# Where two matrices' last columns are decoded: in the attention phase, or in the first steps of the token mix

## The chip, the cores and the metric

One core of a Trainium2 chip runs the kernel; the other cores take no part. The metric is the device time of one execution in microseconds. The kernel before has a median of 588.78 us over three runs (588.4 to 591.17). Names: TensorE is PE in the profile, VectorE is DVE, ScalarE is ACT, GpSimd is POOL, and SyncE, whose queue issues nearly all transfers, is SP.

## The reference

Two stages follow each other. The first is block-sparse attention over 4 batches of 8 heads, 768 positions of 64 elements: a query block of 32 positions sees its neighbours, the first and the last block and three drawn blocks, and the first and last query blocks see everything. The second takes the result as x (4 x 768 x 512):

```python
theta = x @ w_theta
zr, zi = x * np.cos(theta), x * np.sin(theta)
y = np.einsum('ts,bsd->btd', w_tok_r, zr) + np.einsum('ts,bsd->btd', w_tok_i, zi)
u = x + y
return u + np.maximum(u @ w_ch, 0.0)
```

The four weight matrices arrive as 64-bit floating-point numbers (float64 words), 128 partitions wide: w_theta and w_ch have 2048 columns per partition, w_tok_r and w_tok_i 4608 each (six row blocks j of 768). The kernel has to turn each into a pair of 32-bit matrices, a rounded high part and a remainder, and each product is three matmuls: high by high, high by low, low by high.

## The kernel before

**Decoding.** Class `Piece` (L49) turns a run of columns of one matrix into the pair. A piece is loaded as raw words (`raw`, SP, L62), and its work is cut into three phases. *bits* is three VectorE instructions (L71, L72, L73) behind a ScalarE one (L67); *rest* is two on VectorE (L79, L81); *low* is two on VectorE (L90, L91) behind a ScalarE copy that writes the high part (L87). `Decoder` (L94) walks through a list of pieces: `ahead(n)` issues ScalarE's part of the next n phases, `go(n)` VectorE's. Two raw buffers exist, so `go` issues the load of the piece after next behind a *low* (L122).

**Attention.** It works through 52 units: for each of two batch pairs, four wide ones (the first and last query blocks) and 22 regular ones. In a regular unit TensorE makes scores S (L308), VectorE their row minimum m (L310), ScalarE the exponentials P (L319), TensorE transposes them (L325), ScalarE copies the result to pT (L327), and TensorE multiplies with the values into X (L359). Every second unit VectorE normalises two blocks (L340 to L344). GpSimd gathers keys (L269) and values (L291). All of this stands in an order written out by hand, and the engines follow it. Here the first decoder runs: w_theta (4 pieces of 512 columns), then w_tok_r and w_tok_i (9 each). Its 66 phases are dealt out over the units in proportion to weights, by rounding (L493):

```python
phases = round(shares[n] / total * 3 * len(pieces)) - decoder.at
```

A regular unit gets one phase or two. The columns of the token matrices from 1536 on have no place of their own: they are written over buffers that hold keys and values until attention has no more use for them.

**Token mix.** `token_mix` (L585) runs 48 steps k: batch b, half h of the channels, row block j. What a step issues runs ahead of it: `theta(k + 2)` is the matmul with w_theta (L654 to L656), whose left side are the token rows, transposed (`turn`, L637) and cut into two parts (`split`, xTh and xTl, L645 and L646); `reduced`, `waves` and `turned` make the factors zh and zl (L664 to L690); `mix(k)` multiplies them with row block j of the token matrices (L706 to L708). At j = 5 the sum is finished (`add_x`, L713), and `out` (L724) multiplies with w_ch, eight tiles a batch; the tiles of batch 0 are issued in the steps from 13 on. The loads of the tokens, `xa` (L609, four transfers a step) and `xr` (L622), go through SP's queue, in order.

A second decoder takes w_ch in eight pieces of 256 columns. Its first two loads are issued near the end of attention. Steps 0 to 4 (`FIXED`) are part of the hand-written order and run 1, 1, 1, 3 and 3 phases; from step 5 on a scheduler sets the order by its own estimate of times, and three phases are issued in each step from 7 on until all are done.

Of the kernel before, what the change touches and what calls it, by code (L numbers as in the profile page):

```python
# [26 lines left out]
Q_BUFS = 3  # L27
XO_BUFS = 2
FIXED = 5
PHASES = (1, 1, 1, 3, 3)  # L30

# [551 lines left out]
def token_mix(tc, w, ch_pieces, xs, outT, bias, nb, fore):  # L585
# [7 lines left out]
    nc = tc.nc  # L593
    with ExitStack() as late, ExitStack() as ctx:
        half_pi, up_int, down_int, early = bias
# [3 lines left out]
        def at(k):  # L599
            return k // 12, (k // 6) % 2, k % 6  # L600
# [26 lines left out]
        def turn(k, tag="r"):  # L627
            b, h, j = at(k)
            if h:
                return  # L630
            if j % 3 == 0:
                tp = tps[min((2 * b + j // 3) % 3, 1)]
                xT[b, j // 3] = [tp.tile([P, 4, 384], F32R, tag=f"xT{x}", name=f"xT{x}{b}_{j}") for x in "hl"]
            raw = xr.pop((b, j))
            turning[k] = r = xp.tile([P, 4, 128], F32, tag=tag, name=f"r{k}", bufs=3 if tag == "xa" else 1)
            for c in range(4):
                nc.vector.transpose(r[:, c, :].rearrange("p (i t) -> p i t", t=32), raw[:, :, c])  # L637
# [10 lines left out]
        def theta(k):  # L648
            b, h, j = at(k)
            hi, lo = tok(b, j)  # L650
            wh, wl = [x[:, :, 256 * h : 256 * h + 256] for x in w["theta"]]
            angles[k] = ps = ps_h.tile([P, 512], F32, tag="h", name=f"h{k}")[:, 0:256]
            for c in range(4):
                nc.tensor.matmul(ps, hi[:, c, :], wh[:, c, :], start=c == 0, stop=False)  # L654
                nc.tensor.matmul(ps, hi[:, c, :], wl[:, c, :], start=False, stop=False)  # L655
                nc.tensor.matmul(ps, lo[:, c, :], wh[:, c, :], start=False, stop=c == 3)  # L656
# [11 lines left out]
        def waves(k):  # L668
            r = angles[k]
            cs = tz.tile([P, 256], F32, tag="cs", name=f"cs{k}")  # L670
            nc.scalar.activation(cs, r, AF.Abs)  # L671
            nc.scalar.activation(cs, cs, AF.Sin, bias=half_pi, scale=-1.0)
            nc.scalar.activation(r, r, AF.Sin)
            angles[k] = cs, r
# [17 lines left out]
        def turned(k):  # L692
            multiplied(k)
            highs(k)
            lows(k)
# [43 lines left out]
        place = vp.tile([P, 6, 260], F32, tag="vw", name="xr_first").rearrange("p c f -> p (c f)")  # L739
# [5 lines left out]
        decoder = Decoder(ch_pieces(), None, nc.sync, fore)  # L745
# [40 lines left out]
        for k in range(FIXED):  # L786
            theta(k + 2)
            waves(k + 1)
            turn(k + 3)
            turned(k + 1)  # L790
            split(k + 3)
            reduced(k + 2)
            load(k + 3)
            load_raw(k + 5)
            phases = PHASES[k] if k < len(PHASES) else 0
            decoder.ahead(phases)
            decoder.go(phases)
            mix(k)
# [4 lines left out]
        for k in range(FIXED, steps):  # L803
            b, h, j = at(k)
            if k + 4 < steps:
                load(k + 4)
            if k + 5 < steps:
                load_raw(k + 5)
            if k + 2 < steps:
                theta(k + 2)  # L810
                reduced(k + 2)
                waves(k + 2)
                turned(k + 2)
            if k + 3 < steps:
                turn(k + 3)
                split(k + 3)
            if k > 6 and decoder.left():
                decoder.ahead(3)
                decoder.go(3)
            mix(k)  # L820
            if h == 0 and b > 0 and 0 < j < 5:
                for _ in range(2):
                    out(*pending.pop(0), ps_o, "o")
            if h == 1 and j == 5:
                pending += [(b, th, e) for th in range(2) for e in range(4)]
# [4 lines left out]
def sparse_attention_then_token_mix(ctx, tc, qT, qE, kT, vr, sampled, w_theta, w_tok_r, w_tok_i, w_ch, outT):  # L830
    nc = tc.nc
    n_batch = outT.shape[0]
    const = ctx.enter_context(tc.tile_pool(name="const", bufs=1))
    ident = const.tile([P, P], F32, name="ident")
    make_identity(nc, ident)
    bias = []
    for name, value in (("half_pi", math.pi / 2), ("up_int", ROUND), ("down_int", -ROUND), ("early", 0.0)):
        bias.append(const.tile([P, 1], F32, name=name))
        nc.vector.memset(bias[-1], value)
    dram = ctx.enter_context(tc.tile_pool(name="dram", bufs=1, space=bass.MemoryType.DRAM))  # L840
    xs = [dram.tile([NB, 2, 32, 2, 2, P], F32, name=f"xs{bp}") for bp in range(NP)]

    w = {}
    w["theta"] = [const.tile([P, 4, 512], F32R, name=f"w_theta_{x}") for x in ("hi", "lo")]
    for name in ("tok_r", "tok_i"):
        w[name] = [const.tile([P, 2, 768], F32R, name=f"w_{name}_{x}") for x in ("hi", "lo")]

    def room(name, use, dtype=F32):
        return const.tile([P, 8, 768], dtype, tag=f"room_{name}", name=f"{use}_{name}")

    def settle(name):
        t = room(name, "w", F32R)
        w[name] = [x[:, j] for x in w[name] for j in range(2)]
        w[name] = [w[name][2 * x : 2 * x + 2] + [t[:, 4 * x + j] for j in range(4)] for x in range(2)]
        return [t[:, 4 * x : 4 * x + 4] for x in range(2)]

    words = {n: a.bitcast(I32) for n, a in dict(theta=w_theta, tok_r=w_tok_r, tok_i=w_tok_i, ch=w_ch).items()}

    def pieces(name, f, place, at=0, total=3072):
        if place:  # L860
            total = place[0].shape[1] * place[0].shape[2]
        made = []
        for f0 in range(0, total, f):
            made.append(Piece(nc, place, slice(f0, f0 + f), words[name][:, 2 * (at + f0) : 2 * (at + f0 + f)], f"{name}_{at + f0}"))
        return made


    fore = ctx.enter_context(tc.tile_pool(name="fore", bufs=2))
    follow = token_mix(tc, w, lambda: pieces("ch", 256, w["ch"], total=2048), xs, outT, bias, n_batch, fore)
    next(follow)  # L870
    early = pieces("theta", 512, w["theta"])
    early += [x for pair in zip(pieces("tok_r", 512, w["tok_r"]), pieces("tok_i", 512, w["tok_i"])) for x in pair]
    for name in ("tok_r", "tok_i"):
        place = []
        early += pieces(name, 512, place, 1536)
        early[-6].before = lambda name=name, place=place: place.extend(settle(name))
    attention(tc, qT, qE, kT, vr, sampled.bitcast(I32), xs, ident, early, room, follow)
    for _ in follow:
        pass
# [48 lines left out]
```

## Time and profile before

The profiled execution is one of its own: 592.62 us, with a span of 590.8 us from the first instruction to the last, at a mean TensorE clock of 0.991.

| | busy, us | share of the span |
|---|---|---|
| TensorE, matmuls | 538.4 | 91% |
| TensorE, weight loads (beside them) | 475.3 | 80% |
| VectorE | 442.8 | 75% |
| ScalarE | 342.7 | 58% |
| GpSimd | 148.6 | 25% |

Attention is the first 246 us or so; the first product of `mix(0)` starts at 252.9 us. GpSimd works in the first part alone. A busy share is a mean over both parts, so the table by itself says little: the prediction goes by stretches.

In the profile's rows `out<-in` are tile names without their numbers, `x9` is a count, and behind the bar stand the busy time in us, the mean of one instruction in ns, and the idle time of the engine before it with what ended it. A timeline row is start, duration, engine, line, operation. A row of waits is the total, the count and the longest.

### The profile page before, as it was taken

The page shows a single profiled execution, that of the slowest core. Times are in us where ns is not written, and L with a number is a line of the kernel's source. Part 1 is how long each engine was busy: PE and PEld are TensorE (multiplying, and loading weights), DVE is VectorE, ACT ScalarE, POOL GpSimd, SP SyncE. Part 2 cuts the span into 40 slices and gives each one's busy share as a digit, 9 for nine tenths or more (in the row PEclk, how much of TensorE's full clock was granted, in tenths as well). Part 3 has the DMA queues.
Part 4 walks back from the last instruction along what each step waited for, and adds up shares of the span by engine and source line. Part 5 has one row for each costly group of instructions (what it writes and reads, how often), then busy time and mean ns, then how long its engine had stood idle before and what let it go on. Part 6 is the DMA issues. An engine that isn't in the chain of part 4 may idle for free.

```text
span 590.8 us, 16785 instructions
## 1 busy us (share of the span) xinstructions
PE 538.4 (91%) x6636; PEld 475.3 (80%) x6636; DVE 442.8 (75%) x997; ACT 342.7 (58%) x730; POOL 148.6 (25%) x262
## 2 busy tenths in 40 slices
PE   4897878888977977999999999999999999999997
PEld 2564555656645645799999999999999999999996
DVE  3788788878897988888989976648857549547554
ACT  2677666868776876865657443456634547434510
POOL 1477758841775977000000000000000000000000
PEclk9999998999998989999999999999999999999999
DMA  8979999886698998644332341211432111212002
GB/s 293 340 223 344 308 332 348 287 267 223 185 299 257 304 307 225 193 121 131 108 85 76 96 130 59 72 45 54 130 92 70 50 53 42 80 56 75 2 1 107
DMA packets 63263, 95.60 MB, mean 162 GB/s; under 512 B 9168, under 2 KB 44624, under 8 KB 63184
## 3 DMA queue, kind: packets, MB, share of 16 engines
q1 hardware_dynamic: 56848, 71.09, 39.0%
q0 software_dynamic: 6336, 23.43, 12.2%
q8 instruction: 52, 0.85, 0.6%
q14 instruction: 27, 0.22, 0.1%
HBM read 81.90 MB, written 12.58 MB: 160 GB/s over the span
## 4 chain that ended last, share of the span: by engine, by line
PE 68%; DVE 15%; ACT 8%; issue 4%; DMA 4%; SPq 1%; ACTq 0%; DVEq 0%
PE y L706 11%; PE y L707 11%; PE y L708 11%; PE X L359 4%; PE o L730 4%; PE o L729 4%; PE o L731 4%; PE T L325 4%; DVE m L310 3%; PE h L655 3%; PE h L654 3%; PE h L656 3%; ACT P L319 3%; PE S L308 3%; PE SW L401 2%
## 5 line engine op out<-in xcount | busy, mean ns | idle before, releaser
L319 ACT ACTIVATE P<-S,m 128x256 f32<-128x256 f32 x176 | 69.5, 487 | 15.2 <-DVE m L310 15.2
L325 PE MATMUL T<-ident,P 128*128 128x128 f32 x352 | 50.9, 285 | 15.0 <-ACT pT L327 10.4
L310 DVE TENSOR_REDUCE m<-S 128x4 f32<-128x1024 f32 x44 | 53.6, 1217 | 12.3 <-PE S L308 12.3
L327 ACT COPY pT<-T 128x1024 f32<-128x1024 f32 x44 | 44.9, 1021 | 30.5 <-PE T L325 30.4
L325 PEld LDWEIGHTS T<-ident,P 128*128 128x128 f32 x352 | 38.8, 143 | 27.8 <-ACT pT L327 18.3
L291 POOL DMA_INDIRECT vb<-in_vr_dram,rows x44 | 46.3, 1052 | 48.8 <-PE X L359 43.3
L308 PE MATMUL S<-kg,q 64*32 64x256 f32 x1408 | 52.8, 394 | 5.9 <-issue 5.9
L661 ACT ACTIVATE t<-h,up_int 128x256 f32<-128x256 f32 x48 | 22.6, 474 | 59.7 <-PE h L656 56.0
L269 POOL COPY kg<-kb 128x256 f32 (+2 forms) x101 | 50.9, 544 | 15.8 <-PE S L308 15.8
L269 POOL COPY kg<-kb_tok_i 128x256 f32 (+2 forms) x101 | 49.4, 530 | 21.1 <-DMA kb_tok_i<-in_kT_dram 14.9
L654 PE MATMUL h<-w_theta_hi,xTh 128*128 128x256 f32 x192 | 54.1, 282 | 0.4 <-ACT xTh L645 0.4
L656 PE MATMUL h<-w_theta_hi,xTl 128*128 128x256 f32 x192 | 54.1, 282 | 0.2 <-DVE xTl L646 0.2
L655 PE MATMUL h<-w_theta_lo,xTh 128*128 128x256 f32 x192 | 53.9, 281 | 0.0
L706 PE MATMUL y<-w_tok_r,zh 128*128 128x384 f32 x128 | 43.1, 337 | 1.1 <-ACT zh L686 1.1
L706 PE MATMUL y<-w_tok_i,zh 128*128 128x384 f32 x128 | 43.1, 337 | 0.0
L707 PE MATMUL y<-w_tok_r,zh 128*128 128x384 f32 x128 | 43.1, 337 | 0.0
L707 PE MATMUL y<-w_tok_i,zh 128*128 128x384 f32 x128 | 43.1, 336 | 0.0
L708 PE MATMUL y<-w_tok_r,zl 128*128 128x384 f32 x128 | 43.0, 336 | 0.0
L730 PE MATMUL o<-ul,w_ch_hi 128*128 128x384 f32 x128 | 42.9, 335 | 0.0
L731 PE MATMUL o<-uh,w_ch_lo 128*128 128x384 f32 x128 | 42.9, 335 | 0.0
L729 PE MATMUL o<-uh,w_ch_hi 128*128 128x384 f32 x128 | 42.6, 336 | 0.1
L671 ACT ACTIVATE cs<-rr 128x256 f32<-128x256 f32 x48 | 19.7, 414 | 39.1 <-DVE rr L666 38.9
(155 smaller groups left out, 1427.4 us busy)
## 6 DMA issues: line engine op xcount, KB each, us to landing
xa<-xs SPq DMA_DIRECT2D x192, 64.0 KB
out_dram<-of SPq DMA_DIRECT2D x32, 192.0 KB
va<-in_vr_dram SPq DMA_DIRECT2D x22, 260.0 KB
q<-in_qT_dram SPq DMA_DIRECT2D x22, 256.0 KB
xs<-xo SPq DMA_DIRECT2D x88, 64.0 KB
xr<-xs SPq DMA_DIRECT2D x84, 64.0 KB
raw_tok_r<-in_w_tok_r_dram SPq DMA_DIRECT2D x9, 512.0 KB
raw_tok_i<-in_w_tok_i_dram SPq DMA_DIRECT2D x9, 512.0 KB
```

The lines of the kernel that those rows point to most:

```text
L269: nc.gpsimd.tensor_copy(dst, blocks.rearrange("r g s f -> r s g f"))
L308: nc.tensor.matmul(sc[32 * p : 32 * p + 32, e, b, :], q[rows, b, p, :], keys[rows, :, :, place(b, p), :], start=True, stop=True)
L310: nc.vector.tensor_reduce(m, sc, axis=AX.X, op=ALU.min)
L319: nc.scalar.activation(pt[:, e, b, :], sc[:, e, b, :], AF.Exp, bias=m[:, e, b : b + 1], scale=-1.0)
L325: nc.tensor.transpose(t[:, k, :], pt, ident)
L654: nc.tensor.matmul(ps, hi[:, c, :], wh[:, c, :], start=c == 0, stop=False)
L655: nc.tensor.matmul(ps, hi[:, c, :], wl[:, c, :], start=False, stop=False)
L656: nc.tensor.matmul(ps, lo[:, c, :], wh[:, c, :], start=False, stop=c == 3)
L706: nc.tensor.matmul(acc, zh[:, dd], wh[j][:, tt], start=j == 0 and m == 0, stop=False)
L707: nc.tensor.matmul(acc, zh[:, dd], wl[j][:, tt], start=False, stop=False)
L708: nc.tensor.matmul(acc, zl[:, dd], wh[j][:, tt], start=False, stop=j == 5 and m == 1)
L730: nc.tensor.matmul(ps, wh[:, c, :], ul, start=False, stop=False)
```

## The change

The last 512 columns of w_tok_r and of w_tok_i (columns 4096 to 4607, the greater part of row block 5) leave the first decoder. They become four pieces of 256 columns at the head of the second decoder's list, in front of the eight pieces of w_ch. The first decoder has 20 pieces and 60 phases instead of 22 and 66, dealt out over the same units; the second has 12 pieces and 36 phases. `PHASES` now names steps 0 to 12: the token columns take the first twelve phases, which end with step 3, and w_ch takes the rest, up to step 12. The two loads near the end of attention now fetch columns of w_tok_r. All lines from L30 on move down by one.

```diff
-PHASES = (1, 1, 1, 3, 3)
+PHASES = (2, 3, 3, 4, 4, 0, 4, 4, 4, 3, 3, 0, 2)
+LATER = 2560
...
-            phases = PHASES[k] if k < len(PHASES) else 0
+            phases = PHASES[k]
             decoder.ahead(phases)
             decoder.go(phases)
             mix(k)
...
-            if k > 6 and decoder.left():
-                decoder.ahead(3)
-                decoder.go(3)
+            if k < len(PHASES):
+                decoder.ahead(PHASES[k])
+                decoder.go(PHASES[k])
             mix(k)
...
-    follow = token_mix(tc, w, lambda: pieces("ch", 256, w["ch"], total=2048), xs, outT, bias, n_batch, fore)
+    rests = dict(tok_r=[], tok_i=[])
+
+    def mix_pieces():
+        made = [x for n, place in rests.items() for x in pieces(n, 256, place, 1536, (LATER, 3072))]
+        return made + pieces("ch", 256, w["ch"], span=(0, 2048))
+
+    follow = token_mix(tc, w, mix_pieces, xs, outT, bias, n_batch, fore)
...
-    for name in ("tok_r", "tok_i"):
-        place = []
-        early += pieces(name, 512, place, 1536)
-        early[-6].before = lambda name=name, place=place: place.extend(settle(name))
+    for name, place in rests.items():
+        made = pieces(name, 512, place, 1536, (0, LATER))
+        made[0].before = lambda name=name, place=place: place.extend(settle(name))
+        early += made
```

How the instructions move, first on VectorE in attention, late in the first batch pair: from the minimum of unit 20's scores to that of unit 22's. Before:

```order
L310 TENSOR_REDUCE m_20_2018<-S_20_2001 128x4
L71 TENSOR_SCALAR da_tok_i_1999<-da_tok_i_1999 128x512
L72 TENSOR_SCALAR da_tok_i_1999<-da_tok_i_1999 128x512
L73 SCALAR_TENSOR_TENSOR da_tok_i_1999<-raw_tok_i_1815,da_tok_i_1999 128x512
L340 TENSOR_SCALAR sm_17_2089<-X_17_2020 128x8
L341 RECIPROCAL sm_17_2089<-sm_17_2089 128x8
L344 TENSOR_TENSOR xo_17_2092<-X_17_2020,sm_17_2089 128x512
L310 TENSOR_REDUCE m_21_2122<-S_21_2105 128x4
L79 TENSOR_SCALAR ds_tok_i_2139<-da_tok_i_1999 128x512
L81 SCALAR_TENSOR_TENSOR raw_tok_i_1815<-raw_tok_i_1815,ds_tok_i_2139 128x512
L90 TENSOR_TENSOR da_tok_i_1999<-da_tok_i_1999,w_tok_i_hi 128x512
L91 TENSOR_TENSOR w_tok_i_lo<-da_tok_i_1999,raw_tok_i_1815 128x512
```

And of the change, from unit 18's minimum to behind that of unit 20:

```order
L311 TENSOR_REDUCE m_18_1840<-S_18_1823 128x4
L80 TENSOR_SCALAR ds_tok_i_1908<-da_tok_i_1770 128x512
L82 SCALAR_TENSOR_TENSOR raw_tok_i_1572<-raw_tok_i_1572,ds_tok_i_1908 128x512
L341 TENSOR_SCALAR sm_15_1911<-X_15_1842 128x8
L342 RECIPROCAL sm_15_1911<-sm_15_1911 128x8
L345 TENSOR_TENSOR xo_15_1914<-X_15_1842,sm_15_1911 128x512
L311 TENSOR_REDUCE m_19_1951<-S_19_1934 128x4
L91 TENSOR_TENSOR da_tok_i_1770<-da_tok_i_1770,w_tok_i_hi 128x512
L92 TENSOR_TENSOR w_tok_i_lo<-da_tok_i_1770,raw_tok_i_1572 128x512
L311 TENSOR_REDUCE m_20_2005<-S_20_1988 128x4
```

Where two units carried three phases (seven decode instructions), some pairs of units now carry two.

Second, VectorE in the mix, from `reduced(3)` in step 1 to the `split(5)` of step 2, which `theta(5)` on TensorE waits for. Before:

```order
L666 TENSOR_SCALAR rr_4742<-rr_4742 128x256
L79 TENSOR_SCALAR ds_ch_4751<-da_ch_4672 128x256
L81 SCALAR_TENSOR_TENSOR raw_ch_4261<-raw_ch_4261,ds_ch_4751 128x256
L637 STREAM_TRANSPOSE r_4795<-xr_5_4667 128x128 x4
L681 TENSOR_TENSOR cs_4791<-cs_4791,xa_4662 128x256
L681 TENSOR_TENSOR rr_4742<-rr_4742,xa_4662 128x256
L690 TENSOR_TENSOR zl_3_4803<-cs_4791,zh_3_4802 128x256
L690 TENSOR_TENSOR zl_3_4805<-rr_4742,zh_3_4804 128x256
L646 TENSOR_TENSOR xTl_3_4637<-r_4795,xTh_3_4636 128x4x128
```

Of the change:

```order
L667 TENSOR_SCALAR rr_4719<-rr_4719 128x256
L91 TENSOR_TENSOR da_tok_r_4646<-da_tok_r_4646,w_tok_r 128x256
L92 TENSOR_TENSOR w_tok_r<-da_tok_r_4646,raw_tok_r_4235 128x256
L72 TENSOR_SCALAR da_tok_r_4729<-da_tok_r_4729 128x256
L73 TENSOR_SCALAR da_tok_r_4729<-da_tok_r_4729 128x256
L74 SCALAR_TENSOR_TENSOR da_tok_r_4729<-raw_tok_r_4237,da_tok_r_4729 128x256
L80 TENSOR_SCALAR ds_tok_r_4738<-da_tok_r_4729 128x256
L82 SCALAR_TENSOR_TENSOR raw_tok_r_4237<-raw_tok_r_4237,ds_tok_r_4738 128x256
L638 STREAM_TRANSPOSE r_4782<-xr_5_4641 128x128 x4
L682 TENSOR_TENSOR cs_4778<-cs_4778,xa_4636 128x256
L682 TENSOR_TENSOR rr_4719<-rr_4719,xa_4636 128x256
```

Step 1 had one phase (two instructions) in front of the next step's work, and now has three (seven); the two rows on zl and the split follow as before.

More of the change, by code (lines that the diff above doesn't have):

```diff
@@ L857, in sparse_attention_then_token_mix, with pieces @@
     words = {n: a.bitcast(I32) for n, a in dict(theta=w_theta, tok_r=w_tok_r, tok_i=w_tok_i, ch=w_ch).items()}
-    def pieces(name, f, place, at=0, total=3072):
-        if place:
-            total = place[0].shape[1] * place[0].shape[2]
+    def pieces(name, f, place, at=0, span=None):
         made = []
-        for f0 in range(0, total, f):
-            made.append(Piece(nc, place, slice(f0, f0 + f), words[name][:, 2 * (at + f0) : 2 * (at + f0 + f)], f"{name}_{at + f0}"))
+        first, last = span or (0, place[0].shape[1] * place[0].shape[2])
+        for f0 in range(first, last, f):
+            f1 = min(f0 + f, last)
+            made.append(Piece(nc, place, slice(f0, f1), words[name][:, 2 * (at + f0) : 2 * (at + f1)], f"{name}_{at + f0}"))
         return made
     fore = ctx.enter_context(tc.tile_pool(name="fore", bufs=2))
-    follow = token_mix(tc, w, lambda: pieces("ch", 256, w["ch"], total=2048), xs, outT, bias, n_batch, fore)
+    rests = dict(tok_r=[], tok_i=[])
[3 more added lines that the diff above has]
+    follow = token_mix(tc, w, mix_pieces, xs, outT, bias, n_batch, fore)
     next(follow)
```

## The prediction

> **What bounds the kernel now.** I read the page's slices first, then busy time by stage, then what TensorE waits for, then the chain of waits.
>
> ```profile
> span 590.8 us, 16785 instructions
> PE   4897878888977977999999999999999999999997
> DVE  3788788878897988888989976648857549547554
> DMA  8979999886698998644332341211432111212002
> ...
> core 0: us, PE busy (x) PEld busy (x) DVE busy (x) ACT busy (x) POOL busy (x), PEclk, DMA share, GB/s
> 0.00:246.00 246.00, 199.97 (x4439) 138.67 (x4440) 197.75 (x336) 173.51 (x324) 148.57 (x262) 0.98 0.89 281
> 246.00:345.00 99.00, 96.75 (x701) 95.34 (x700) 88.08 (x263) 60.95 (x154) 0.00 (x0) 1.00 0.37 105
> 345.00:591.00 246.00, 241.64 (x1501) 241.32 (x1500) 156.97 (x400) 108.25 (x253) 0.00 (x0) 1.00 0.21 65
> ...
> PE y L706 <- ACT zh L686: 1.1, 1, 1.1
> ...
> 252.90 0.41 PE L706 MATMUL y<-w_tok_r_hi,zh 128*128 128x384 f32 x1 [0.34 <-DVE xo L344]
> ```
>
> There are two programs in one. Attention (to about 246 us) has no full engine: TensorE 200.0, VectorE 197.8, ScalarE 173.5 of 246, and the DMA engines at 0.89. The mix behind it, whose first product starts at 252.90, is TensorE's: the list of its waits from there on holds one of 1.1 us and that one of 0.3, so whatever is moved there is free only while VectorE and ScalarE stay ahead. Until 345 us they hardly are: VectorE is busy 88.08 of 99. After 345 it has 246 - 157 = 89 us to spare.
>
> In attention the chain of waits changes hands. Two stretches, and VectorE's busy time in those where it carries the chain:
>
> ```profile
> by line: DVE m L310 34.5%; DVE da_tok_i L73 11.1%; DVE da_tok_i L71 8.2%; DVE da_tok_i L90 7.6%; DVE w_tok_i L91 7.3%; DVE raw_tok_i L81 7.3%; DVE da_tok_i L72 7.3%; DVE xo L344 6.9%; DVE ds_tok_i L79 3.9%; issue 2.4%; ACT P L319 2.4%; DVE
> by line: PE X L359 21.1%; PE S L308 20.0%; PE T L325 19.1%; issue 13.3%; ACT pT L327 8.4%; ACT P L319 7.5%; DVE m L310 7.2%; PE X L366 3.5%; DVE da_tok_i L90 1.8%; DVE w_tok_i L91 0.8%; ACTq L327 0.1%
> ...
> 28.00:52.00 24.00, 21.78 (x36) 1.00 0.82 247
> 105.00:124.00 19.00, 17.39 (x28) 1.00 0.87 270
> 186.00:206.00 20.00, 19.41 (x30) 1.00 0.94 285
> ```
>
> The first row is the chain from 186 to 206 us: half of it (11.1 + 8.2 + 7.6 + 7.3 + 7.3 + 7.3 + 3.9 = 52.7%) is decoding of w_tok_i. There VectorE is busy 19.41 of 20 us, and a phase less is time less. The second row is 206 to 240 us: scores, transposes and values carry it, and decoding has 2.6%. So VectorE sets the pace in about 63 of the 210 us that decode.
>
> **The change, part 1: what leaves attention.** Two pieces of 512 columns, one of each token matrix, with their two loads of 512 KB. What one costs:
>
> ```profile
> L73 DVE SCALAR_TENSOR_TENSOR da_tok_i<-raw_tok_i,da_tok_i 128x512 int32<-128x512 int32 x9 | 6.6, 738 | 0.3
> L81 DVE SCALAR_TENSOR_TENSOR raw_tok_i<-raw_tok_i,ds_tok_i 128x512 f32<-128x512 uint32 x9 | 6.5, 726 | 0.3
> L91 DVE TENSOR_TENSOR w_tok_i<-da_tok_i,raw_tok_i 128x512 fp32r<-128x512 f32 x6 | 5.6, 940 | 0.3
> L71 DVE TENSOR_SCALAR da_tok_i<-da_tok_i 128x512 f32<-128x512 f32 x9 | 5.0, 551 | 2.4 <-ACT da_tok_i L67 2.4
> L90 DVE TENSOR_TENSOR da_tok_i<-da_tok_i,w_tok_i 128x512 f32<-128x512 f32 x6 | 4.6, 773 | 0.0
> L79 DVE TENSOR_SCALAR ds_tok_i<-da_tok_i 128x512 int32<-128x512 int32 x9 | 4.4, 487 | 0.1
> L72 DVE TENSOR_SCALAR da_tok_i<-da_tok_i 128x512 int32<-128x512 int32 x9 | 4.2, 468 | 0.3
> ...
> L310 DVE TENSOR_REDUCE m<-S 128x4 f32<-128x1024 f32 x44 | 53.6, 1217 | 12.3 <-PE S L308 12.3
> ```
>
> VectorE: 738 + 726 + 940 + 551 + 773 + 487 + 468 = 4.68 us a piece, 1.56 us a phase. So 9.4 us of VectorE go, and ScalarE's two instructions a piece. But 60 phases instead of 66 are dealt out over the same units, so it is not the last stretch that empties: by the rounding, 14 units lose a phase and 8 gain one, six fewer in all. One net phase falls into each of the three full stretches quoted: 3 x 1.56 = 4.7 us. The other three fall where TensorE, instruction issue or a transfer carries the chain; I give them 0.2 us each. Sum **-5.3 us**. Bounds: if only one full stretch pays, -1.5. At the other end, the 44 row minima (L310) mark the units' starts: of 19 pairs of regular units, the 15 with three phases took 9.2 us on the mean, the 4 with two 7.1. That is 2.1 us a phase, and six of them -12.5 us. I stay near the low end because the longer pairs also hold the waits for transfers, which no phase causes. The loads (2 x 512 KB at 281 GB/s, 3.7 us of a DMA queue that is 0.89 busy) pull the same way and are not counted again.
>
> **Part 2: what comes to the mix.** The same columns in four pieces of 256, before any of w_ch, so that steps 0 to 4 now run 16 phases instead of 9 and w_ch ends in step 12.
>
> ```profile
> L81 DVE SCALAR_TENSOR_TENSOR raw_ch<-raw_ch,ds_ch 128x256 f32<-128x256 uint32 x8 | 3.4, 422 | 0.1
> L73 DVE SCALAR_TENSOR_TENSOR da_ch<-raw_ch,da_ch 128x256 int32<-128x256 int32 x8 | 3.4, 420 | 0.1
> L90 DVE TENSOR_TENSOR da_ch<-da_ch,w_ch_hi 128x256 f32<-128x256 f32 x8 | 3.4, 420 | 0.2 <-ACT xTh L645 0.2
> L91 DVE TENSOR_TENSOR w_ch_lo<-da_ch,raw_ch 128x256 fp32r<-128x256 f32 x8 | 3.4, 419 | 0.0
> L71 DVE TENSOR_SCALAR da_ch<-da_ch 128x256 f32<-128x256 f32 x8 | 2.3, 291 | 2.1 <-ACT da_ch L67 2.1
> L79 DVE TENSOR_SCALAR ds_ch<-da_ch 128x256 int32<-128x256 int32 x8 | 2.3, 289 | 0.1
> L72 DVE TENSOR_SCALAR da_ch<-da_ch 128x256 int32<-128x256 int32 x8 | 2.2, 284 | 0.0
> ```
>
> A piece is 2.55 us by its durations. In the queue instructions overlap a little: in the timeline below, the six from L72 to the next stage's L681 take 280.33 - 278.12 = 2.21 us, with L71 about 2.4, or 0.8 a phase. Four pieces are 9.6 us (10.2 by durations) on an engine that was idle 99 - 88 = 11 us until 345. All of it fits by then; the question is what it delays on the way.
>
> ```profile
> 266.33 0.69 DVE L646 TENSOR_TENSOR xTl<-r,xTh 128x512 fp32r<-128x512 f32 x1
> 278.12 0.25 DVE L72 TENSOR_SCALAR da_ch<-da_ch 128x256 int32<-128x256 int32 x1
> 280.33 0.42 DVE L681 TENSOR_TENSOR cs<-cs,xa 128x256 f32<-128x256 f32 x1
> 290.41 0.42 DVE L690 TENSOR_TENSOR zl<-rr,zh 128x256 fp32r<-128x256 f32 x1
> ...
> 268.55 0.28 PE L656 MATMUL h<-w_theta_hi,xTl 128*128 128x256 f32 x1
> 291.65 0.51 PE L708 MATMUL y<-w_tok_i_hi,zl 128*128 128x384 f32 x2
> ...
> DVE r L637 <- DMA xr<-xs: 1.4, 2, 0.9
> ```
>
> First place: theta(5). Its token rows are ready at 266.33 + 0.69 = 267.02 and first used at 268.55, 1.5 us in hand. By the order VectorE now has five phases ahead of them instead of two, 3 x 0.8 = 2.4 us more, so TensorE stands 0.9. Second place: mix(6). Its last factor is ready at 290.41 + 0.42 = 290.83 and used at 291.65, 0.8 in hand. Ahead of it, counted from mix step 0, the order has 36 decode instructions where there were 23, seven to a piece: 13/7 x 2.4 = 4.5 us. The two waits for raw x rows (1.4) are swallowed, because VectorE comes later to them. That leaves 4.5 - 0.8 - 1.4 = 2.3 us, in which the 0.9 is contained. TensorE's 1.1 us stall of before comes behind this place and is partly covered by it, so I take **+2.0 us**. Behind the late instructions queue the next stage's multiplications and, in order, all of mix(7) to mix(12). Lower bound 0, if VectorE's other short waits go too; upper bound +7, all 9.6 us less the 0.8 in hand, the 1.4 and a part of the old stall.
>
> Two more things are late next.
>
> ```profile
> 317.22 0.42 DVE L91 TENSOR_TENSOR w_ch_lo<-da_ch,raw_ch 128x256 fp32r<-128x256 f32 x1
> ...
> 342.16 0.34 PE L729 MATMUL o<-uh,w_ch_hi 128*128 128x384 f32 x1
> ...
> 296.02 0.44 ACT L67 ACTIVATE da_ch<-raw_ch 128x256 f32<-128x256 f32 x1 [3.41 <-DMA raw_ch<-in_w_ch_dram]
> ```
>
> The last piece of w_ch was ready at 317.6, and the first output tile that needs it began at 342.16, 24 us in hand. Now it is due in step 12, and the order has it behind the factors of mix(14): a few microseconds stay, and I cost it at nothing. The four added loads go through SP's queue, each behind the VectorE instruction that frees its buffer, and the loads of xa and xr behind it wait too. The third row shows the worst that was: ScalarE stood 3.41 us for a raw piece. In the new order the third to sixth load are issued in steps 1 to 3, a step ahead of their use; I count 0 to 0.6 us, inside the +2.0.
>
> The Trainium skill's page "VectorE: DVE Perf Modes" (section "The TRN2 errata — SBUF-src ops pay a fixed extra latency per instruction") speaks against halving the pieces: every instruction pays a fixed cost, and it advises 512 elements or more. The trace agrees in the durations, 2 x 2.55 = 5.09 us for two halves against 4.68 for a whole. By the rule the exchange costs 2 x 0.4 = 0.8 us of VectorE time more, and the sum below would end at -2.5; I go by the 2.4 us that a piece holds the queue, where that cost is mostly overlapped.
>
> **Sum.** -5.3 + 2.0 = -3.3 us. Made against the profiled execution (592.6 us by its own time, span 590.8) this is 589.3. That execution lies 3.8 above the median of the runs, which I forecast as 588.8 - 3.3 = **585.5 us**.
>
> **Rivals.**
> A. VectorE paces all of attention: the 2.1 us a phase of the pairs is real everywhere. -10 to -12.5, +2.0: about 579.5. For it: decode is half of VectorE's work there. Against: the chain from 206 to 240 us.
> B. Attention does not follow VectorE: its end is set by TensorE's 200 us, by transfers (0.89 busy) and by issue, and the freed time reappears as waits for scores. -1.5 to -2 and +2: 588.8. For it: the second chain row. Against: 19.41 of 20.
> C. Slower: VectorE's queue from the end of step 1 to mix(6) becomes the bound. If its waits there are not swallowed, because they are ScalarE's latencies and late raw pieces, the whole upper bound of +7 falls on TensorE; with -4 from attention that gives +3, 592 us. It decides if theta(5) already comes over 2 us late, where I count 0.9. For it: 88 of 99 us busy. Against: before, steps 3 and 4 ran three phases each without a stall.
> D. The order doesn't do what the table says: after step 4 a scheduler places the phases, and if VectorE is 4 us later than I count, the last w_ch piece holds the output matmuls of step 13. Those 4 us on top: 589.5.
>
> **Chances.** Forecast 0.45 (its own range 582.8 to 587.8), A 0.13, B 0.27, C 0.13, D 0.02. What a measurement can tell here is about 0.5%, 2.9 us. Faster by more than that (below 585.8): 0.6 of the forecast's 0.45, all of A, a tenth of B, together 0.43. Slower by more: most of C, a little of B, 0.13. Within: 0.44. The range reaches to 580, the edge of A, and up to 591, short of C's middle.
>
> **What would show it.** Right: attention's end (the first L706) comes about 5 us earlier than 252.9; in the full stretches VectorE stays the chain, with fewer decode rows; from the first L706 to the end the kernel takes 1 to 3 us longer than 337.9, with new waits of TensorE for xTl or xTh before theta(5) and for z before mix(6). Wrong: the first L706 hardly moves (B), or TensorE's waits between steps 3 and 9 sum to over 5 us (C).

## The result, and the profile after

The changed kernel takes 587.68 us (median of 21 runs, 582.58 to 591.83) beside 589.26 us for the kernel before (21 runs, 586.58 to 599.42). The ratio is 0.9949 with a 95% interval of 0.9925 to 0.9972: 3.0 us faster, between 1.6 and 4.4. The forecast was 3.3. The ratios leave out disturbed runs, so they are not always the quotient of the two medians beside them, and the profiled execution of the change, 591.45 us, is one of those left out: it is read stage by stage and beside other executions of the same kernel, not by its total.

Page of the change, the span and busy tenths of 40 slices:

```profile
span 589.7 us, 16811 instructions
PE   4898887998988978989999999999999999999997
DVE  2687985887889878889989996648857549547554
```

Its busy time by stage, columns as in the prediction's first fence:

```profile
0.00:246.00 246.00, 206.92 (x4562) 145.88 (x4563) 193.48 (x340) 177.41 (x333) 150.66 (x262) 0.97 0.88 280
246.00:345.00 99.00, 93.63 (x585) 90.81 (x584) 89.28 (x274) 58.85 (x150) 0.00 (x0) 1.00 0.39 109
345.00:591.00 246.00, 240.60 (x1493) 240.28 (x1491) 157.25 (x401) 107.80 (x252) 0.00 (x0) 1.00 0.21 65
```

In the first 246 us TensorE now does 206.92 us of work instead of 199.97, while VectorE does 193.48 instead of 197.75: attention now ends inside this window. From 246 to 345 us it is the other way round, 93.63 instead of 96.75.

Where the two stages meet shows in the first products of three mix steps. Timeline of TensorE in the change: the first products of mix(0), mix(8) and mix(24).

```profile
245.61 0.41 PE L707 MATMUL y<-w_tok_r_hi,zh 128*128 128x384 f32 x1 [0.33 <-DVE xo L345]
...
299.34 0.33 PE L707 MATMUL y<-w_tok_r,zh 128*128 128x384 f32 x1
...
404.95 0.34 PE L707 MATMUL y<-w_tok_r_hi,zh 128*128 128x384 f32 x1
```

And in the kernel before, mix(8) and mix(24) (mix(0), at 252.90, stands in the prediction):

```profile
303.29 0.45 PE L706 MATMUL y<-w_tok_r,zh 128*128 128x384 f32 x1 [1.12 <-ACT zh L686]
...
405.98 0.34 PE L706 MATMUL y<-w_tok_r_hi,zh 128*128 128x384 f32 x1
```

In these two executions attention ends 252.9 - 245.6 = 7.3 us earlier. (In other executions with the change's attention it ends up to 6 us earlier still; the last section has the spread.) Then 3.3 us are given back up to mix(8) (53.7 instead of 50.4 us after the first product) and another 3.0 up to mix(24) (159.3 instead of 153.1 us). Behind that nothing more is lost: 344.1 us from the first product to the end against 337.9.

The list of what TensorE waited for says where. In the change, 246 to 345 us (total, count, longest):

```profile
PE y L707 <- ACT zh L687: 2.2, 2, 1.4
PE h L655 <- ACT xTh L646: 1.7, 2, 0.9
PE h L657 <- DVE xTl L647: 0.4, 2, 0.2
PE o L731 <- DVE ul L723: 0.4, 1, 0.4
PE y L707 <- DVE uf L720: 0.4, 1, 0.4
PE y L709 <- DVE zl L691: 0.2, 1, 0.2
```

The longest in the first row is the first product of mix(5). The second row is theta(4) and theta(5). The other 0.9 us of the first row and the last three lie in steps 12 to 14. The list adds up to 5.3 us, but the mix became some 6 us longer. The next fence, TensorE around theta(4), shows why such gaps cost more than their size:

```profile
255.08 0.34 PE L708 MATMUL y<-w_tok_i_lo,zh 128*128 128x384 f32 x1
255.25 0.34 PE L709 MATMUL y<-w_tok_i_hi,zl 128*128 128x384 f32 x1
256.53 0.39 PE L655 MATMUL h<-w_theta_hi,xTh 128*128 128x256 f32 x1 [0.94 <-ACT xTh L646]
256.75 0.28 PE L656 MATMUL h<-w_theta_lo,xTh 128*128 128x256 f32 x1
257.25 0.39 PE L657 MATMUL h<-w_theta_hi,xTl 128*128 128x256 f32 x1 [0.22 <-DVE xTl L647]
```

Products normally start 0.17 us apart though each lasts 0.34, so that two overlap. The gap is counted from the end of the one before: from 255.25 to 256.53 pass 1.28 us where 0.17 would do, a loss of 1.1 and not 0.94.

Attention lost its VectorE stretch. The chain of waits of the change from 186 to 206 us, and below it the same stretch in a second execution of the same kernel (`e0_change_again`, 586.61 us):

```profile
by line: POOL kg L270 60.7%; issue 20.3%; POOLq L260 11.7%; POOL vb L292 9.5%; POOLq L270 2.8%; POOLq L292 0.2%
...
by line: ACT P L320 19.8%; issue 15.2%; ACT pT L328 11.1%; PE T L326 11.0%; PE X L360 10.1%; PE S L309 8.2%; DVE m L311 5.7%; DVE da_tok_i L91 4.1%; DVE raw_tok_i L82 3.8%; DVE w_tok_i L92 3.6%; ACT w_tok_i L88 3.2%; DVE ds_tok_i L80 2.6%; 
```

And its busy time in the three stretches that the prediction called full:

```profile
28.00:52.00 24.00, 21.85 (x532) 15.58 (x531) 21.30 (x37) 19.93 (x40) 16.80 (x28) 1.00 0.76 237
105.00:124.00 19.00, 18.10 (x479) 12.96 (x464) 16.51 (x25) 15.10 (x32) 14.15 (x23) 1.00 0.82 244
186.00:206.00 20.00, 17.65 (x466) 12.43 (x454) 18.12 (x28) 15.73 (x32) 18.18 (x30) 1.00 0.99 309
```

Where half the chain was decoding, it is now 14% in e0's row (4.1 + 3.8 + 3.6 + 2.6) and nothing in the other. What took over differs by execution: GpSimd's gathers of keys (L270) have 60.7% in the one and nothing in e0, where ScalarE and TensorE share the chain; of the five further profiled executions with the change's attention and its decoding in the mix, two have some 50% of such gathers (e4, f1), one 18% (f0) and two none (e5, f2). VectorE is down from 19.41 to 18.12 of 20 us.

### The profile page after: what moved, and what is told of

It is laid out like the page before. It is cut to its first block, busy times and chain, and to the rows that moved or that the text cites. A ratio compares the mean times of both kernels' runs of the same rounds, so it can differ in the third digit from the quotient of the medians.

```text
span 589.7 us, 16811 instructions
## 1 busy us (share of the span) xinstructions
PE 541.2 (92%) x6636; PEld 477.0 (81%) x6636; DVE 440.0 (75%) x1011; ACT 344.1 (58%) x734; POOL 150.7 (26%) x262
## 4 chain that ended last, share of the span: by engine, by line
PE 59%; DVE 15%; issue 6%; POOL 6%; ACT 5%; DMA 3%; POOLq 2%; SPq 2%; DVEq 0%; ACTq 0%
PE y L709 8%; PE y L707 8%; PE y L708 8%; POOL kg L270 5%; PE o L731 4%; PE o L732 4%; PE o L730 4%; PE T L326 4%; PE X L360 3%; PE S L309 3%; PE h L657 3%; PE h L655 3%; PE h L656 3%; PE SW L402 2%; DVE m L311 2%
## 5 line engine op out<-in xcount | busy, mean ns | idle before, releaser
L326 PE MATMUL T<-ident,P 128*128 128x128 f32 x352 | 52.5, 291 | 9.3 <-ACT P L320 3.2
L270 POOL COPY kg<-kb 128x256 f32 (+2 forms) x101 | 53.3, 569 | 16.2 <-PE S L309 16.1
L270 POOL COPY kg<-kb_tok_i 128x256 f32 (+2 forms) x101 | 50.8, 543 | 25.2 <-DVE sb_scratch L176 15.2
L326 PEld LDWEIGHTS T<-ident,P 128*128 128x128 f32 x352 | 40.3, 147 | 21.0 <-ACT pT L328 10.9
L309 PE MATMUL S<-kg,q 64*32 64x256 f32 x1408 | 51.0, 393 | 3.7 <-issue 2.2
L292 POOL DMA_INDIRECT vb<-in_vr_dram,rows x44 | 44.5, 1012 | 37.3 <-PE X L360 31.2
```

The lines of the kernel that those rows point to most:

```text
L270: nc.gpsimd.tensor_copy(dst, blocks.rearrange("r g s f -> r s g f"))
L309: nc.tensor.matmul(sc[32 * p : 32 * p + 32, e, b, :], q[rows, b, p, :], keys[rows, :, :, place(b, p), :], start=True, stop=True)
L326: nc.tensor.transpose(t[:, k, :], pt, ident)
```

## The experiments

The theory after the result: attention gains more than forecast, because decoding on VectorE holds it in more places than three, and the mix gives back more than forecast. Rivals: for attention, that it is the transfers (two loads of 512 KB less) and not VectorE; for the mix, that the loss comes with a mere shift of attention's end and not with the decoding. Each kernel was timed beside the kernel before; where the last 512 columns are filled with a constant, they are not decoded anywhere.

**The change again, and each half of it alone.** `e0_change_again` is the changed kernel. `e1_attention_alone` has its attention, and the mix's order of before; the last 512 columns are filled with a constant by GpSimd:

```diff
-PHASES = (2, 3, 3, 4, 4, 0, 4, 4, 4, 3, 3, 0, 2)
+PHASES = (1, 1, 1, 3, 3)
...
+        for name in ("tok_r", "tok_i"):
+            for x in w[name]:
+                nc.gpsimd.memset(x[5][:, 256:768].bitcast(F32), 0.03125)
...
-            if k < len(PHASES):
-                decoder.ahead(PHASES[k])
-                decoder.go(PHASES[k])
+            if k > 6 and decoder.left():
+                decoder.ahead(3)
+                decoder.go(3)
...
-        return made + pieces("ch", 256, w["ch"], span=(0, 2048))
+        return pieces("ch", 256, w["ch"], span=(0, 2048))
```

`e2_mix_alone` decodes everything in attention as before, and the same columns once more in the change's order of the mix:

```diff
-        made = pieces(name, 512, place, 1536, (0, LATER))
+        made = pieces(name, 512, place, 1536, (0, 3072))
```

`e4_gentle` is the change with another order of phases:

```diff
-PHASES = (2, 3, 3, 4, 4, 0, 4, 4, 4, 3, 3, 0, 2)
+PHASES = (2, 2, 2, 3, 3, 0, 3, 3, 3, 3, 3, 3, 3, 3)
```

> The changed kernel itself, beside the others on the same chip, for a second profile. -3.0 us against before; if the 6.1 us that its first profile lost behind the first product are a property of the kernel and not of that execution, this profile again has 343 to 345 us there, and waits of TensorE before theta(4), theta(5) and mix(6) of about 1 us each.

> The attention half of the change alone: 20 pieces are decoded in attention as in the change, the mix is that of the kernel before (its own order, word for word), and the last 512 columns of both token matrices are not decoded at all: GpSimd, idle in the mix, fills them with a constant, so the result is not the reference's. My sum says 5.3 us faster than before (first product of the mix near 247.6 us instead of 252.9, mix as long as before, 337.9). The profiles of before and of the change, taken by themselves, say 7.3 faster. The rival that attention does not follow VectorE says 1.5 to 2 faster.

> The mix half alone: attention decodes all 22 pieces as before, and the mix decodes the same last 512 columns a second time, in the change's own order, into the same place. My sum says 2.0 us slower than before. The profiles, taken by themselves, say 6.1 slower (344.1 instead of 337.9 from the first product on). The rival in which VectorE is the bound of the mix says 5 to 7. If the two halves add up, this and the first run together give the change's own difference, about -3.0.

> The change with 2, 2, 2, 3, 3 phases in steps 0 to 4 and 3 each in steps 6 to 13, so that the token columns are still ready for mix(5) and w_ch ends one step later. My theory of the mix (VectorE's queue ahead of theta(5) and mix(6)) says that the wait before theta(5) falls by about 0.8 us and the one before mix(6) by about as much: 1 to 2 us faster than the change, unless the output matmuls of step 13 now wait for w_ch (rival D: 2 us slower than the change).

Measured, against 590.94 us of the kernel before:

| | median, us | ratio, 95% interval | difference, us |
|---|---|---|---|
| e0_change_again | 589.14 | 0.9968 (0.9937 to 1.0000) | -1.9 |
| e1_attention_alone | 582.54 | 0.9877 (0.9831 to 0.9924) | -7.3 |
| e2_mix_alone | 594.79 | 1.0057 (1.0031 to 1.0083) | +3.4 |
| e4_gentle | 587.74 | 0.9934 (0.9897 to 0.9971) | -3.9 |

The halves add up, -7.3 + 3.4 = -3.9, to what the change gives within its intervals. By these middle values the forecast of -5.3 + 2.0 had both terms too small, by 2.0 and 1.4, and the errors partly cancelled; the intervals (4.5 to 10.0 and 1.8 to 4.9) exclude neither term. The loss comes without any gain in attention: in e2 attention is that of before and ends when it did (252.2 us), and the mix still takes 342.3 us. e0's profile bears out what the first one showed: 343.3 us behind the first product, with waits of 1.06 us at theta(4), 0.79 at theta(5) and 1.37 at mix(5), where mix(6) was expected. In e4 the wait of mix(5) for zh is gone, and another has come in its place. TensorE's waits in e4 from 246 to 330 us:

```profile
PE y L707 <- ACT w_tok_i L88: 1.6, 1, 1.6
PE y L707 <- ACT zh L687: 0.9, 1, 0.9
PE h L657 <- DVE xTl L647: 0.7, 3, 0.2
PE h L655 <- ACT xTh L646: 0.6, 1, 0.6
```

The whole last token piece falls into step 4 there, and mix(5) meets it three quarters through. That e4 is faster than the change can't be told from their intervals.

**What attention gained: VectorE or the transfers.** All on top of e1. `e8_loads_back` puts four loads of 256 KB back into SP's queue, which nobody reads:

```diff
+            if k % 3 == 2 and self.pool is self.raws and k // 3 in (3, 7, 11, 15):
+                again = self.raws.tile([P, 256, 2], I32, tag="again", name=f"again_{k}", bufs=1)
+                self.queue.dma_start(again, self.pieces[k // 3].src[:, 0:512].rearrange("p (f w) -> p f w", w=2))
```

`e9_vector_back` repeats the VectorE instructions of a phase in six places, on tiles that are done with (`again` issues those of one phase with `da` as input and output); `e10_both_back` has both edits.

```diff
+            if k % 3 == 2 and self.pool is self.raws and k // 3 in (2, 5, 8, 11, 14, 17):
+                piece.again(("bits", "rest", "low")[(k // 3 // 3) % 3])
```

`e7_four_pieces_out` takes four pieces out instead of two and fills the last 1024 columns with a constant:

```diff
-LATER = 2560
+LATER = 2048
...
-                nc.gpsimd.memset(x[5][:, 256:768].bitcast(F32), 0.03125)
+                nc.gpsimd.memset(x[4][:, 512:768].bitcast(F32), 0.03125)
+                nc.gpsimd.memset(x[5][:, 0:768].bitcast(F32), 0.03125)
```

> Attention alone with two pieces out, and four loads of 256 KB put back into SP's queue in attention (the bytes of the two pieces; nobody reads them). The last 512 columns are filled with a constant and not decoded. Theory that the saved time is VectorE's: these loads change nothing, 7 us below the kernel before, ratio 0.987 to 0.989. Rival, that it is the transfers (1 MB less in a stage whose transfer engines are 0.88 busy): all or most of the gain goes, ratio 0.995 to 1.0.

> Attention alone with two pieces out, and VectorE's 14 instructions of two pieces put back in six places of one phase each, on tiles that are done with (no load, no ScalarE copy). The last 512 columns are filled with a constant and not decoded. Theory that the saved time is VectorE's: most of the 7.3 us is lost again, ratio 0.996 to 1.0. Rival (transfers, ScalarE): nothing is lost, ratio 0.987 to 0.989.

> Attention alone with two pieces out, and both the 14 VectorE instructions and the four loads of 256 KB put back (the last 512 columns are filled with a constant and not decoded). With VectorE's work alone the ratio was 0.996, with the loads alone 0.9885, with neither 0.988. Theory that VectorE's work is all that counts and the 2.5 us left over is scatter or placing: 0.995 to 0.997 again. Rival, that the transfers count too once VectorE is full: 0.999 to 1.001, all of the gain gone.

> Attention alone as in the run with two pieces taken out, but with four pieces out (the last 1024 columns of both token matrices are filled with a constant and not decoded; the mix is that of the kernel before). Theory that VectorE sets attention's pace phase by phase: two more pieces are worth again 6 phases of 1.2 us, so 14 to 15 us below the kernel before, ratio 0.975 to 0.977. Rival, that another engine (GpSimd with its gathers, TensorE, ScalarE) takes over as soon as two pieces are out: 8 to 10 us below, ratio 0.983 to 0.986, with the chain of waits through that engine.

Measured on one chip, against 594.25 us of the kernel before (e10: 593.64):

| | median, us | ratio, 95% interval | difference, us |
|---|---|---|---|
| e8_loads_back | 586.92 | 0.9885 (0.9850 to 0.9919) | -6.8 |
| e9_vector_back | 590.88 | 0.9958 (0.9928 to 0.9989) | -2.5 |
| e10_both_back | 593.00 | 1.0014 (0.9978 to 1.0050) | +0.8 |
| e7_four_pieces_out | 583.79 | 0.9852 (0.9807 to 0.9897) | -8.8 |

e1 was timed on another chip, so the kernels of this table are best compared with each other. With the loads back and VectorE's work gone, 6.8 us are gained, as much as e1 gained within the intervals: no loss by the loads alone shows. With VectorE's work back and the loads gone, 2.5 are left, and the intervals of e8 and e9 lie apart. So 4.3 us, most of the gain, are VectorE's. What the remaining 2.5 us are is open. e10 has both back and nothing is left, but its interval overlaps with e9's, and the profiles don't put the difference into attention: the first product of the mix comes at 255.1 us in e9 and at 249.6 in e10, and it is the mix, the same code in both, that takes 337.2 and 340.3 us. That transfers cost time beside a full VectorE is not shown.

Two more pieces out bring 2.0 us more than e8 (1.5 more than e1 on its chip), not 7: after the first six phases VectorE no longer sets the pace alone, as the rival had it. That one certain engine takes over is not shown: from 186 to 206 us the chain of e7 is again largely VectorE's (its row minima have 28.3%, and decoding much of the rest), and that of e1 TensorE's. The busy time of the first 240 us of e1, and what VectorE waited for there from 28 us on:

```profile
0.00:240.00 240.00, 204.10 (x4531) 141.93 (x4533) 190.49 (x330) 175.69 (x329) 150.44 (x266) 0.99 0.91 286
```

```profile
DVE m L311 <- PE S L309: 14.1, 10, 2.7
...
DVE sm L341 <- PE X L360: 2.5, 3, 1.5
```

And the same two views of e7:

```profile
0.00:240.00 240.00, 202.44 (x4535) 141.35 (x4537) 184.18 (x317) 173.65 (x325) 147.75 (x270) 0.99 0.88 281
```

```profile
DVE m L311 <- PE S L309: 12.1, 11, 2.6
DVE sm L341 <- PE X L360: 6.3, 5, 2.1
```

In these two executions VectorE does 6.3 us less and TensorE has got no further (202.44 against 204.10); for TensorE's scores and sums together VectorE waits 18.4 us instead of 16.6.

**Why theta(4) waited.** The prediction did not look at this place, and TensorE stood there 0.94 us. ScalarE's and VectorE's rows of the change in step 0, and behind them SP's queue:

```profile
251.74 0.43 ACT L68 ACTIVATE da_tok_r<-raw_tok_r 128x256 f32<-128x256 f32 x1 [2.91 <-DMA xs<-xo]
...
252.20 0.29 DVE L72 TENSOR_SCALAR da_tok_r<-da_tok_r 128x256 f32<-128x256 f32 x1 [2.12 <-ACT da_tok_r L68]
...
244.82 1.77 SPq L379 DMA_DIRECT2D xs<-xo  x4
246.69 1.86 SPq L610 DMA_DIRECT2D xa<-xs  x4
248.65 1.76 SPq L379 DMA_DIRECT2D xs<-xo  x4
```

The first decode instruction of the mix (ScalarE's Abs, L68) waits for a store of attention's last result, with which it has nothing to do: the decoder's scratch (`da`, `ds`, pool stage2) is laid over the memory of the buffer xo. SP issues four transfers in about 1.8 us, and the last stores go out at 248.65 behind loads of xa and xr. Behind the waiting instruction stand VectorE's whole step and `turn(4)`. The kernel before had the same wait for its first piece of w_ch; ScalarE's row of it, from 253 to 262 us:

```profile
ACT da_ch L67 <- DMA xs<-xo: 1.1, 1, 1.1
```

`e5_other_room` moves the scratch, in the change:

```diff
         tps.append(late.enter_context(tc.tile_pool(name="tp1", bufs=2)))
+        decoder.pool = late.enter_context(tc.tile_pool(name="stage2", bufs=1))
...
-        decoder.pool = late.enter_context(tc.tile_pool(name="stage2", bufs=1))
```

> The change, with the decoder's scratch of the mix (da, ds) allocated right behind tp1, so that its first Abs no longer takes the memory of attention's last xo and no longer waits for the stores of it (2.91 us of ScalarE and 2.12 us of VectorE in the change's step 0). Theory: that wait delays turn(4) and xTh of step 4, and theta(4) stands 0.94 us for it. Then the wait in front of the first Abs is under 0.5 us, theta(4) has no wait over 0.3 us for xTh, and the time is 1 to 1.5 us below the change: ratio to the kernel before about 0.993. Rival: VectorE is late there because two and three phases of decoding stand in steps 0 and 1 at all: the first Abs waits less, but theta(4) still stands 0.6 to 0.9 us, ratio 0.995 to 0.997.

585.65 us against 594.25, ratio 0.9887 (0.9843 to 0.9932). ScalarE no longer waits in front of the first Abs, VectorE 0.2 us for issue, and theta(4) has no wait; theta(5) keeps 0.52 and mix(5) 1.38. The waits went as the theory says, and the time fell further than they explain, so the kernel was run once more, beside the change:

> The changed kernel itself, beside the two below on one chip: ratio to the kernel before 0.995 to 0.997 as in its two earlier comparisons, with TensorE waits of 0.94 at theta(4), 0.78 at theta(5) and 1.38 at mix(5).

> The change with the decoder's scratch allocated behind tp1, a second time, beside the change. If the 3 us seen between the two on different chips are this edit's, ratio 0.989 to 0.991 to the kernel before, and 0.994 to the change. By its waits alone (0.94 + 0.22 + 0.26 of TensorE's waits gone, with the lost overlap about 1.8 us) it should be 0.993 and 0.997.

Against 593.88 us: the change 588.93 us, 0.9936 (0.9908 to 0.9964); with the scratch moved 587.60 us, 0.9904 (0.9871 to 0.9938). Side by side the two can't be told apart. The profile of this execution of the change says why it may be so; ScalarE's row:

```profile
ACT da_tok_r L68 <- DMA xs<-xo: 0.8, 1, 0.8
```

In f0 the store came in time, the wait was 0.8 us, VectorE lost nothing by it and theta(4) did not wait, against what was expected of it; theta(5) waited 0.36 us and mix(5) 1.37. The mix took 341.3 us, and 341.8 with the scratch moved. In the change's two other profiled executions the wait was 2.9 and 3.0 us and the mix took 344.1 and 343.3. So the wait is worth about 2 us in some executions and nothing in others; how often, the runs don't settle.

**The waits that are left.** They should follow from how many decode instructions stand ahead on VectorE. In e5, VectorE ahead of z(5), for which mix(5) waits:

```profile
267.38 0.42 DVE L91 TENSOR_TENSOR da_tok_i<-da_tok_i,w_tok_i 128x256 f32<-128x256 f32 x1
...
268.17 0.29 DVE L72 TENSOR_SCALAR da_tok_i<-da_tok_i 128x256 f32<-128x256 f32 x1
...
270.75 0.42 DVE L682 TENSOR_TENSOR cs<-cs,xa 128x256 f32<-128x256 f32 x1
...
271.66 0.44 PE L707 MATMUL y<-w_tok_r,zh 128*128 128x384 f32 x1 [1.38 <-ACT zh L687]
```

From 267.38 to 270.75 VectorE does nothing but decode. `f2_respaced` is e5 with

```diff
-PHASES = (2, 3, 3, 4, 4, 0, 4, 4, 4, 3, 3, 0, 2)
+PHASES = (1, 2, 4, 3, 3, 4, 4, 3, 3, 3, 3, 3)
```

> The same, with the phases of the mix dealt out as 1, 2, 4, 3, 3, 4, 4, 3, 3, 3, 3, 3. Theory that the waits follow the number of decode instructions ahead on VectorE: ahead of theta(5)'s rows stand 3 phases instead of 5 (1.6 us less), so its 0.52 us wait goes; ahead of z(5) stand 24 instructions instead of 28 (4 x 0.34 = 1.4 us less), so the 1.38 us wait of mix(5) at its start goes; in exchange the last piece of w_tok_i comes behind the sums of mix(5)'s first two products, and TensorE waits 1.3 to 1.6 us for it three quarters through mix(5). Sum within 1 us of the run without this. Rival, that these waits come from ScalarE's order or from late raw pieces: both waits stay within 0.3 us of 0.52 and 1.38.

587.30 us, ratio 0.9864 (0.9835 to 0.9893), beside f0 and f1. TensorE's waits in f2, from 245 us to the end:

```profile
PE h L655 <- ACT xTh L646: 1.6, 1, 1.6
PE y L707 <- ACT zh L687: 1.4, 2, 1.0
PE o L730 <- ACT w_ch_hi L88: 0.5, 1, 0.5
```

theta(5) waits no more, as the theory has it. mix(5) waits 1.0 instead of 1.38, less of a change than the 1.4 expected; mix(4) has a new wait of 0.4, and the expected one for w_tok_i did not show. The 1.6 us are later, in step 14. So the count of instructions holds for theta(5), and for z(5) only in part: the scheduler, which orders everything from step 5 on, also moves other work when the phases move.

f2 is 8.1 us below the kernel before (6.4 to 9.8), and its interval lies below that of the change on the same chip, though not below f1's. Against the change the margin is thin: by the medians of all runs f2, f1 and f0 take 587.30, 587.60 and 588.93 us. Its profile shows no gain over them either: its mix takes 341.4 us, the same as f0's and f1's. That f2 is faster than those two is not secure.

**Where the mix loses.** By how much mix(k) starts later than in the kernel before, in us, each counted from the first product of its own mix; worked out from the starts of the first of 24 products of each step, as in the rows of mix(8) and mix(24) above. "Store" is how long ScalarE's first decode instruction waited for the store of xo (1.1 us in the kernel before). The last column is when the last instruction on w_ch (L92) ends, from the same zero:

```
                     store  mix(2) mix(3) mix(8) mix(16) mix(24)  end   w_ch done
the change             2.9   +1.7   +3.2   +3.3    +6.4    +6.3  +6.1        94.5
e0_change_again        3.0   +1.8   +3.4   +3.4    +5.7    +5.5  +5.4        93.7
f0_change_beside       0.8    0.0   +1.1   +1.1    +3.7    +3.5  +3.4        91.7
e2_mix_alone           2.0   +0.7   +2.3   +2.3    +5.1    +4.9  +4.3        93.1
e5_other_room         none    0.0   +1.3   +1.5    +4.2    +4.1  +3.9        92.2
f2_respaced           none    0.0    0.0   +0.9    +1.6    +3.6  +3.5        92.4
e1_attention_alone     2.4   +0.4   +0.4   +1.6    +1.5    +1.5  +0.8        65.7
e9_vector_back         1.2    0.0    0.0    0.0     0.0     0.0  -0.7        65.1
e10_both_back          2.5   +0.6   +0.6   +2.3    +2.3    +2.3  +2.3        66.3
```

The first two columns of starts are theta(4) and theta(5). Up to mix(8) the loss goes with the store. In the mix of before it is 0.0 where that wait is short (1.2 us in e9) and 1.6 and 2.3 where it is long (e1, e10). In the mix of the change it is 0.9 to 1.5 without the wait or with a short one, and 3.3 and 3.4 with a long one. So some 2 us of the loss there go with the store's wait, in either mix, and about 1 us comes with the decoding of token columns.

Then the kernels that decode token columns in the mix lose another 2.1 to 3.0 us between mix(8) and mix(24), and the three with the mix of before lose nothing there. What sets them apart is the last column: w_ch is done some 65 us after the first product in the one kind (64.7 in the kernel before: 317.22 + 0.42 - 252.90) and some 93 in the other, in the middle of the sums and factors of steps 11 to 14. That holds for f2 too, though its table ends with step 11: the scheduler puts the phases later than the step that issues them. VectorE from 67 to 87 us after the first product, in f0 and in the kernel before, and the product of f0 that waits at the end of it, the first of mix(14):

```profile
312.80:332.80 20.00, 19.73 (x61) 1.00 0.27 74
...
319.90:339.90 20.00, 18.56 (x52) 1.00 0.31 93
...
331.56 0.44 PE L707 MATMUL y<-w_tok_r,zh 128*128 128x384 f32 x1 [0.86 <-ACT zh L687]
```

VectorE is full there in f0. From 313.8 us to 331.24, where the product that ScalarE turns into zh starts, it has no gap, and 16 of its instructions are on w_ch; in the kernel before none is.

## Why the prediction was right or wrong

**The time** was right: 587.7 for 585.5, or -3.0 for -3.3 us, inside the range. It lies just inside the forecast's own range (582.8 to 587.8) too. But by what the halves gave alone both terms were too small, and that their errors partly cancelled was luck.

**Attention, -5.3: too small, measured -7.3** (4.5 to 10.0; with the loads put back -6.8). The weak step is "The other three fall where TensorE, instruction issue or a transfer carries the chain; I give them 0.2 us each". 7.3 over six phases is 1.2 us each, not 0.9 on the mean; the interval, 0.75 to 1.7, still holds both. The price of a phase in a full stretch, 1.56, was not tested by itself, but rival A with its 2.1 fell: the interval ends at 10.0, where A began, and e7 shows that the slope ends after two pieces. That the loads needn't be counted held as far as it goes: alone they cost nothing that shows (e8). Rival B fell with e1 and e9. The first product came 7.3 us earlier where 5 were forecast; but "in the full stretches VectorE stays the chain" is wrong for 186 to 206 us, where it passed to GpSimd in one execution and to ScalarE and TensorE in another.

**The mix, +2.0: too small, measured +3.4** (1.8 to 4.9), and 3.4 to 6.1 in the profiled executions of the change.
- theta(5), "TensorE stands 0.9": measured 0.78 + 0.22 in the change, 0.52 + 0.22 without the store's wait. Right.
- "Second place: mix(6)": the wait came at mix(5), 1.38 us. I had compared the decode instructions ahead of mix(6), 36 for 23; ahead of z(5) the order has 28 for 14, the larger growth, and that place comes first. The size, 2.3 less the 0.9 contained in it, was 1.4.
- theta(4) was not priced. The prediction named SP's queue, but looked only at the raw loads in it, "0 to 0.6 us"; the store of xo for which the scratch waits was in the profile before as a wait of 1.1 us. It costs 0 to about 2 us, by execution, and it does so in the mix of before too.
- "The last w_ch piece ... I cost it at nothing": here the larger part of the miss lies. The piece itself was in time. But decoding that goes on to 93 us instead of 65 stands between the sums and factors of steps 12 to 14 on VectorE, and the table shows 2.1 to 3.0 us lost there in each kernel of this kind. That these phases do it follows from what the kernels have in common and from VectorE's full stretch in f0; no kernel without them in these steps and with the rest of the change was run.
- The 2.4 us that a piece holds VectorE's queue: in e5's rows one takes 270.75 - 268.17 = 2.58 us, so two halves hold it 5.16 us against 4.68 for a whole by durations, and the overlap that I counted on is not there. That is nearer to the Trainium skill's rule that every instruction pays a fixed cost ("VectorE: DVE Perf Modes", section "The TRN2 errata — SBUF-src ops pay a fixed extra latency per instruction"). Its sum of -2.5 and the measured -3.0 (1.6 to 4.4) don't contradict each other.

**Rival C** did not come: the waits between steps 3 and 9 add up to 0.78 + 0.22 + 1.38 = 2.4 us, under the 5 named. But "1 to 3 us longer than 337.9" was wrong, it was 3.4 to 6.1. D, a late last piece, did not come; the delay around it did.

## What to carry to other kernels

When work is moved from an early stage to a later one, price both ends by the place and not by busy shares: for each engine that the bound engine waits for, count the instructions that the new order puts ahead of every point where something is handed over, and take the first such point, not the one that looks tightest in the old trace. Look also at the last steps that the moved work now reaches, and at what its scratch memory was used for just before. And a forecast that comes out right in the sum is worth taking apart, because its halves can be run alone.

## What the runs showed of the hardware that was not expected

- Transfers and VectorE together: 1 MB of loads put back beside a VectorE with room cost nothing that shows (0.9885 with them, 0.9877 without, on two chips). Beside a full VectorE the ratio was 1.0014 with them and 0.9958 without; these intervals overlap.
- The same kernel's first decode instruction of the mix waited 0.8, 2.9 and 3.0 us for a store issued behind loads in SP's queue, in three executions.
- A gap in TensorE's row understates the loss by 0.17 us where products overlap: 0.94 recorded, 1.11 lost.
- The granted clock differed between kernels: on one chip e8 had 0.9903 on the mean of its runs, and e9 with VectorE's instructions in place of the loads 0.9843 (standard errors 0.0013 and 0.0012). Within the runs of a kernel 0.01 of clock goes with about 2.5 us, so 1.5 of the 4 us between the two go with the clock. Which is the cause of which was not tested. In the profile of the change the lowered clock lies in attention (0.97 up to 246 us, 1.00 behind).
- Seven profiled executions with the change's attention had their first product between 239.4 and 245.8 us: attention scatters by 6 us from execution to execution. From mix(24) to the end the kernels of the table agree within 0.7 us.
